# Adding the odd running sums of two units onto the even ones, clearing pads in part, and new engine orders in a gated linear attention with a ReGLU layer

## The chip, the core and the metric

One core of one Trainium2 chip runs the whole program. The metric is the device time of one execution in microseconds (us). Three executions of the kernel before took 193.5, 193.56 and 193.87 us: the median is 193.56 us.

## What is computed

For 4 sequences (batch B), 8 heads of width 48 and 768 tokens, a gated linear attention runs over the tokens, and its output, 3072 rows of 384, passes a ReGLU feed-forward layer:

```python
f = 1.0 / (1.0 + np.exp(-f_logit))
for t in range(S):
    state = f[:, :, t, :, None] * state + np.einsum('bhd,bhe->bhde', k[:, :, t], v[:, :, t])
    y[:, :, t] = np.einsum('bhd,bhde->bhe', q[:, :, t], state)
x = y.transpose(0, 2, 1, 3).reshape(B * S, H * D)
out = (np.maximum(x @ w_gate, 0.0) * (x @ w_val)) @ w_out     # 384 -> 1536 -> 384
```

Inputs and output are float32.

## The kernel before

The recurrence is worked in chunks of 128 tokens. Within a chunk, b(t) is the running sum of -log f, kept in bf16 as `bneg`; k is scaled by exp(b), q by exp(-b) (the "hats"), and masked products of the two give the part within the chunk, while a state of 48 x 48 per head carries the rest on. There are six groups c = 0 to 5 of four positions b = 0 to 3, 128 rows each, so 512 rows a group. Groups 0 and 1 are made of four **units**: a unit takes the first 256 tokens of one sequence, with tokens 2p and 2p+1 on partition p. Its two positions are the even tokens (b even) and the odd tokens (b odd). The change speaks of units 3 and 4: counted from zero they are 2 and 3, that is group 1, positions 0 and 1, and positions 2 and 3.

Every piece of work has a short name, which the text uses; digits are group and position:

- `Lf, Lk, Lq, Lv`: loads of an input (lines 406 and 411), 384 KB each. `wg0+2` and the like: loads of slices of w_gate, w_val, w_out from column block 0, two blocks (line 431, POOL queue).
- `ef`, `ln` (ACT, lines 478 and 481): exp, then log(1+x), for both positions of a unit at once.
- `cum` (PE, `cum2`, lines 492 to 500): the running sums, into one PSUM bank; the even position also sums the decays of its two chunks (line 498). `ek`, `eq` (ACT, 516 and 518) are the exponentials of the sums, `dc` (526) those of the decays. They read that bank.
- `hk`, `hq` (POOL or DVE, 540 and 541): k and q times the exponentials. `tk`, `tq` (PE, 552): their transposes; `ck`, `cq` (DVE or ACT, 556 and 557): the copies from PSUM.
- `s` (PE, 650): scores of a unit into four banks; `m` (DVE, 657): the masked copies. `y` (672), `yi` (708): outputs within and across chunks; `x` (597, ACT or DVE): their copy, the feed-forward layer's input. `v`: copy of v into `vpad` (570 to 572). `kv` (695), `st`, `ss`, `sd` (450 to 456): states.
- `g`, `u` (PE, 792): gate and value products of a hidden block j; `r` (ACT or DVE, 797 and 798): relu; `p` (DVE, 800): the product of the two. `o` (813), `d` (819 and 820), `S` (823): output product, copy, store. g00.2 is group 0, first position 0, block 2. Blocks 0 to 3 of group 0 are worked for two positions at a time (256 columns: g00.j, g02.j), all others for four (512 columns).

The order on each engine is written out in tables: `ORDER` lists operations by number for each engine, a negative entry ~7512 on PE means 7 products of 512 columns of zeros (line 877), which compute nothing. Before such a run, PE waits until the bank it writes is free. `BANKS` gives a bank for each accumulator in the order in which PE opens them. `HELD` adds waits: a load with a number in it waits until another has landed. All other waits follow from what an operation reads and writes; an operation that writes a bank waits for all readers of the bank's last use. The engines run these lists in order, so whatever waits holds all that stands behind it.

Of the kernel before, what the change touches and what calls it, by code (L numbers as in the profile page):

```python
# [14 lines left out]
X_WAY = "t" * 16 + "x" * 8  # L15
RUNS = {(c, b) for c in range(6) for b in (0, 2)}
# [8 lines left out]
        45, ~60100, 76, 87, ~4512, 84, ~3512, 92, 82, 103, ~2512, 94, 123, 112, 97, ~7512, 120, ~2512, 130, 102, 128, 106,  # L25
        118, 139, 158, 133, 154, 232, 243, ~3512, 150, 152, 146, 138, 279, 268, 142, 156, 160, 148, 174, 176, 170, 172, 186,
# [13 lines left out]
    ],  # L40
    "ACT": [
# [8 lines left out]
    ],  # L50
    "DVE": [
# [12 lines left out]
    ],  # L64
    "POOL": [
# [4 lines left out]
    ],  # L70
# [9 lines left out]
    51: 53, 57: 58, 59: 63, 63: 58, 65: 69, 67: 71, 70: 50, 71: 60, 72: 54, 517: 68,  # L80
# [161 lines left out]
def bass_hgrn2_outer__then__ffn_reglu_kernel(  # L242
# [10 lines left out]
    B, H, S, D = q.shape  # L253
# [106 lines left out]
    for i in range(NH):  # L360
        fill("DVE" if i < 3 else "POOL", f"hats{i}", hats[:, i, :, :, D:64], 0.0, 256, -14 + i)
    for i in range(NV):
        fill("POOL", f"vpad{i}", vpad[i][:], 0.0, VW, -8 + i)
# [95 lines left out]

    def halves(n, slot):  # L460
        return rows_of(n, slot).rearrange("p h (i d) -> p i h d", i=2)

    def front(c, b):
# [26 lines left out]
        bc = Bank("a")  # L490

        def cum2():
            for i in range(2):
                x = te.matmul(bc.ap[:, 0:HD], tsum[i * (1 - bj)][:, :], bneg[:, bi, i, :, 0:D], start=(i == 0), stop=(i == 1), skip_group_check=True)  # L494
            if bj == 0:
                for p in range(NP):
                    for i in range(2):
                        x = te.matmul(bc.ap[:, HD + 2 * p:HD + 2 * p + 2], bneg[:, bi, i, 2 * p:2 * p + 2, :].rearrange("p h d -> p (h d)"), pair[:, :],
                                      start=False, stop=(i == 1), skip_group_check=True)
            return x  # L500
# [442 lines left out]
```

## Time and profile before

| | before |
|---|---|
| median of three runs | 193.56 us |
| the profiled execution, whole | 193.41 us |
| its span, first to last instruction | 191.7 us |
| granted TensorE clock, mean | 1.000 |
| PE busy | 186.0 us in 2006 products |
| DVE, ACT, POOL busy | 146.7, 83.4, 60.0 us |

The profile is a page on one execution, taken by the hardware. Its other views, used below, are a timeline (start and length in us, engine, line, operation, shapes; behind a number in brackets, how long the engine had been idle and for whom it waited), busy times in chosen stretches, groups of instructions by line, and the chain of work that ended last, followed back. Lengths of neighbouring instructions of one engine overlap, since an engine is a pipeline: the distance from one start to the next is called a pitch below.

### The profile page before, as it was taken

To read this page: it belongs to the slowest core of one execution; us is meant where nothing else is said; L and a number is where in the kernel's file an instruction comes from. 1 tells how busy PE (TensorE), PEld (TensorE's weight loads), DVE (VectorE), ACT (ScalarE), POOL (GpSimd) and SP (SyncE) were. 2 spreads that over 40 slices of the span, in tenths; PEclk is the share of its full clock that TensorE was granted. 3 is DMA by queue.
4 is the path that set the end of the run, shared out by engine and by line. 5 is a ranking of instruction groups with operands and counts; after the bars stand their busy time and mean duration, and the time that the engine had idled before them with its cause. 6 is when DMAs were issued, how large, how long until landed. Compare 5 with 4: busy or idle time off the path is not lost.

```text
span 191.7 us, 4882 instructions
## 1 busy us (share of the span) xinstructions
PE 186.0 (97%) x2006; PEld 109.7 (57%) x2006; DVE 146.7 (77%) x264; ACT 83.4 (44%) x183; POOL 60.0 (31%) x92
## 2 busy tenths in 40 slices
PE   7899999999999999999999999999999999999994
PEld 7555675565645556655455755556555565555553
DVE  4469946999768989879986789996888947677331
ACT  2776963520387780472213996513351220222211
POOL 8899320201055820368200283911180000000000
DMA  5999999999989999899999999993239010000413
GB/s 149 325 285 261 206 208 278 204 225 279 241 185 193 225 212 208 160 187 255 204 162 220 238 203 236 176 202 79 64 120 180 20 41 3 2 0 0 164 44 123
DMA packets 110311, 32.44 MB, mean 169 GB/s; under 512 B 103504, under 2 KB 110032, under 8 KB 110288
## 3 DMA queue, kind: packets, MB, share of 16 engines
q1 hardware_dynamic: 95120, 25.44, 62.4%
q0 software_dynamic: 3776, 3.54, 11.4%
q10 hardware_dynamic: 11392, 3.15, 7.4%
q8 instruction: 16, 0.26, 0.6%
q14 instruction: 7, 0.06, 0.1%
HBM read 25.95 MB, written 4.72 MB: 160 GB/s over the span
## 4 chain that ended last, share of the span: by engine, by line
PE 75%; DMA 10%; DVE 5%; ACT 5%; issue 1%; POOL 1%; SPq 1%; ACTq 0%
PE ps L792 40%; PE ps L813 24%; DMA f_in<-in_f_logit_dram 7%; DMA wg<-in_moe_w_gate_dram 3%; PE ps L584 2%; DVE gT L800 2%; DVE hats L541 2%; PE ps L745 1%; PE ps L672 1%; PE ps L503 1%; POOL hats L540 1%; ACT f_in L478 1%; ACT expo L518 1%; PE ps L756 1%; ACT bneg L481 1%
## 5 line engine op out<-in xcount | busy, mean ns | idle before, releaser
L800 DVE TENSOR_TENSOR gT<-relu,ps 128x512 bf16<-128x512 bf16 (+1 forms) x76 | 48.5, 654 | 15.4 <-PE ps L792 11.4
L792 PE MATMUL ps<-xT,wg 128*128 128x512 bf16 (+1 forms) x228 | 57.8, 368 | 0.1
L792 PE MATMUL ps<-xT,wv 128*128 128x512 bf16 (+1 forms) x228 | 57.5, 368 | 0.0
L813 PE MATMUL ps<-wo,gT 128*128 128x384 bf16 (+2 forms) x300 | 51.9, 320 | 0.2 <-DVE gT L800 0.2
L797 ACT ACTIVATE relu<-ps 128x512 bf16<-128x512 f32 (+1 forms) x39 | 21.8, 565 | 46.2 <-PE ps L792 26.6
L813 PEld LDWEIGHTS ps<-wo,gT 128*128 128x128 bf16 x300 | 27.1, 98 | 18.4 <-DVE gT L800 1.2
L792 PEld LDWEIGHTS ps<-xT,wv 128*128 128x128 bf16 x228 | 23.6, 108 | 19.7 <-ACT expo L518 0.3
L792 PEld LDWEIGHTS ps<-xT,wg 128*128 128x128 bf16 x228 | 23.3, 108 | 19.1 <-DMA wg<-in_moe_w_gate_dram 0.6
L798 DVE TENSOR_SCALAR relu<-ps 128x512 bf16<-128x512 f32 (+1 forms) x37 | 24.8, 673 | 5.4 <-PE ps L792 4.4
L570 POOL CAST vpad<-v_in 128x384 bf16<-128x384 f32 x14 | 7.5, 550 | 43.6 <-PE ps L745 22.4
L592 DVE TENSOR_TENSOR ptm<-ps,tri 128x512 bf16<-128x512 f32 x32 | 19.9, 680 | 1.3 <-PE ps L584 1.3
L540 POOL TENSOR_TENSOR hats<-q_in,expo 128x384 bf16<-128x384 f32 x14 | 14.5, 1045 | 9.5 <-ACT expo L518 8.7
L478 ACT ACTIVATE f_in<-f_in 128x768 f32<-128x768 f32 x12 | 10.1, 845 | 14.1 <-DMA f_in<-in_f_logit_dram 14.0
L540 POOL TENSOR_TENSOR hats<-k_in,expo 128x384 bf16<-128x384 f32 x13 | 13.8, 1071 | 7.0 <-ACT expo L516 3.8
L456 POOL TENSOR_TENSOR st<-ssum,dec 128x384 bf16<-128x384 f32 x11 | 9.7, 878 | 16.1 <-DVE ssum L454 16.1
L518 ACT ACTIVATE expo<-ps 128x384 f32<-128x384 f32 x24 | 11.7, 492 | 4.2 <-PE ps L503 2.9
L597 ACT ACTIVATE xT<-ps 128x384 bf16<-128x384 f32 x10 | 5.4, 548 | 16.9 <-PE ps L672 8.3
L516 ACT ACTIVATE expo<-ps 128x384 f32<-128x384 f32 x24 | 11.6, 493 | 1.1 <-PE ps L494 0.6
L819 ACT ACTIVATE osb<-ps 128x384 f32<-128x384 f32 (+1 forms) x15 | 7.3, 483 | 10.3 <-PE ps L813 9.8
L657 DVE TENSOR_TENSOR ptm<-ps,tmask 128x512 bf16<-128x512 f32 x16 | 10.2, 681 | 1.2 <-PE ps L650 1.1
L877 PE MATMUL ps<-zeros 128*128 128x100 bf16 (+1 forms) x81 | 10.6, 307 | 0.0
L481 ACT ACTIVATE bneg<-f_in 128x768 bf16<-128x768 f32 x12 | 10.1, 842 | 0.2
(78 smaller groups left out, 169.8 us busy)
## 6 DMA issues: line engine op xcount, KB each, us to landing
out_dram<-osb SPq DMA_DIRECT2D x23, 192.0 KB, 2.4
f_in<-in_f_logit_dram SPq DMA_DIRECT2D x11, 384.0 KB, 5.9
k_in<-in_k_dram SPq DMA_DIRECT2D x11, 384.0 KB, 5.7
q_in<-in_q_dram SPq DMA_DIRECT2D x10, 384.0 KB, 5.7
v_in<-in_v_dram SPq DMA_DIRECT2D x8, 384.0 KB, 5.1
v_in<-in_v_dram ACTq DMA_DIRECT2D x4, 384.0 KB, 6.4
q_in<-in_q_dram ACTq DMA_DIRECT2D x2, 384.0 KB, 6.5
wg<-in_moe_w_gate_dram POOLq DMA_DIRECT2D x2, 384.0 KB, 8.8
```

What stands on the lines that cost most here:

```text
L478: add(f"ef{c}{b0}", by("ACT", lambda: sc.activation(raw, raw, AF.Exp, scale=-1.0), act_(n)), keys, keys, key=P)
L481: add(f"ln{c}{b0}", by("ACT", lambda: sc.activation(bo, fl, AF.Ln, bias=1.0), act_(n)), keys + [f"bneg{bi}"], [f"bn{bi}_{x % 2}" for x in ...
L516: add(f"ek{c}{b}", by("ACT", lambda: sc.activation(ex[:, 1, :], bc.ap[:, 0:HD], AF.Exp, scale=1.0), act_(HD)), [bc], [f"expk{ei}"], key=P + 1)
L518: add(f"eq{c}{b}", by("ACT", lambda: sc.activation(ex[:, 0, :], bc.ap[:, 0:HD], AF.Exp, scale=-1.0), act_(HD)), [bc], [f"expq{ei}"], key=P ...
L540: return {**by("POOL", lambda: gp.tensor_tensor(o, i_, e_, ALU.mult), pool_(HD)), **by("DVE", lambda: ve.tensor_tensor(o, i_, e_, ALU.mult ...
L592: add(f"m{c}{b}{j}", by("DVE", lambda b=b, j=j, mi=mi: ve.tensor_tensor(ptm[mi][:, j, :, :], s[b, j].ap[:, :].rearrange("p (n t) -> p n t" ...
L792: z = te.matmul(bank.ap[:, 0:n], wt[:, kt, w_cols(j)], xT[xi][:, kt, n0:n1], start=(kt == 0), stop=(kt == NK - 1))
L797: add(f"r{c}{b0}.{j}", {**by("ACT", lambda: sc.activation(rdst, gate.ap[:, 0:n], AF.Relu), act_(n)), **by("DVE", lambda: ve.tensor_scalar_ ...
L798: **by("DVE", lambda: ve.tensor_scalar_max(rdst, gate.ap[:, 0:n], 0.0), dve_(n))}, [gate], [f"relu{ri}"], key=P)
L800: add(f"p{c}{b0}.{j}", by("DVE", lambda: ve.tensor_tensor(gT[gi][:, j, n0:n1], rdst, val.ap[:, 0:n], ALU.mult), dve_(n)), [val, f"relu{ri} ...
L813: z = te.matmul(o.ap[:, 0:e1 - e0], gT[gi][:, j, b * C:(b + 1) * C], wo[:, j, e0:e1], start=(j == 0), stop=(j == NJ - 1))
L877: te.matmul((op.opens[0].ap if op.opens else banks[7])[:, 0:fill % 1000], zeros[:, 0:128], zeros[:, 0:fill % 1000], start=True, stop=True, ...
```

## The change

For units 3 and 4, the sums of the odd tokens are no longer two products into a bank of their own (sum of the even gates and sum of the odd gates up to the token). One product with the identity adds the odd gates onto the even sums, in the bank where these lie. It stands behind all readers of the even sums (`ek`, `eq` and `dc`), since it overwrites what they read. w_out stays in its four slices (`WO` is as it was). Of `vpad`, only the 64 columns of pads that no copy fills are cleared, not all 448, still on POOL; all six `hats` pads are cleared on DVE, where three were POOL's. All five orders, `BANKS` and `HELD` are new.

```diff
+ONTO = {2, 3}
...
-        fill("DVE" if i < 3 else "POOL", f"hats{i}", hats[:, i, :, :, D:64], 0.0, 256, -14 + i)
+        fill("DVE", f"hats{i}", hats[:, i, :, :, D:64], 0.0, 256, -14 + i)
...
-        fill("POOL", f"vpad{i}", vpad[i][:], 0.0, VW, -8 + i)
+        fill("POOL", f"vpad{i}", vpad[i][:].rearrange("p (n e) -> p n e", n=NP)[:, :, D:64], 0.0, 64, -8 + i)
...
-        bc = Bank("a")
+        onto = two and bj and w // 2 in ONTO
+        bc = sums_at[w // 2] if onto else Bank("a")
+        sums_at[w // 2] = bc
         def cum2():
+            if onto:
+                return te.matmul(bc.ap[:, 0:HD], ident[:, :], bneg[:, bi, 1, :, 0:D], start=False, stop=True, skip_group_check=True)
...
-            add(f"cum{c}{b}", pe(cum2, mm(HD) * 2 + (mm(2) * 8 if bj == 0 else 0)), ["tsum0", "tsum1", "pair", f"bneg{bi}", f"bn{bi}_0", f"bn{bi}_1"],
-                [bc], key=P, opens=[bc])
+            add(f"cum{c}{b}", pe(cum2, mm(HD) if onto else mm(HD) * 2 + (mm(2) * 8 if bj == 0 else 0)),
+                ["ident", f"bneg{bi}", f"bn{bi}_1"] if onto else ["tsum0", "tsum1", "pair", f"bneg{bi}", f"bn{bi}_0", f"bn{bi}_1"],
+                [bc], key=P, opens=[] if onto else [bc])
```

The orders are given by name up to the place where both kernels have done the same work on PE. PE before, then after:

```
warm ~60x100 cum00 cum01 ~4 tq00 ~3 tk01 tk00 kv00 ~2 tq01 cum03 cum02 s00 ~7 tq02 ~2 tq03 y00 tk03 yi01 tk02 kv02
  g00.3 s02 g00.2 cum10 cum11 ~3 g00.1 u00.1 g00.0 y02 cum13 cum12 yi03 u00.2 u00.3 u00.0 | g02.3 u02.3 ...
warm ~60x100 cum00 cum01 ~7 tq00 ~2 tq01 tk00 tk01 kv00 ~5 cum02 s00 cum03 ~3 tq02 ~2 tq03 ~1 y00 yi01 tk02 tk03 kv02
  g00.3 s02 g00.2 g00.0 u00.0 ~3 cum10 g00.1 u00.1 cum12 y02 u00.3 u00.2 yi03 cum11 cum13 | g02.1 g02.0 u02.0 g00.4 g02.3
  u02.3 tq12 g00.7 u02.1 u00.4 g00.5 u00.7 u00.5 g02.2 u02.2 g00.6 u00.6 ~1 tk10 ~1 g00.8 ...
```

Here ~7 stands for 7 empty products of 512 columns. Behind the bar PE has no empty products before, and two after. The other engines in the same stretch, after:

```
ACT  ef00 ln00 dc00 eq00 eq01 ek01 ek00 cq00 ef02 ck01 ln02 ck00 eq02 dc02 ek02 eq03 ek03 cq02 x01 ck02 ef10 ln10 r00.2
     ef12 r00.0 ln12 eq10 ek10 dc10 r00.1 eq12 dc12 x02 ek12 x03 eq11 ek11 ...
DVE  ... hk00 hk01 cq01 st00 ss10 v03 sd10 m000 m011 m001 m010 cq03 hk02 hk03 x00 ck03 st01 r00.3 ss11 m031 m030 m021
     p00.0 m020 p00.1 p00.3 p00.2 ...
POOL ... wg2+2 ... v01 v00 hq00 hq01 wo0+2 wv0+2 v02 wg0+2 hq02 hq03 wv2+2 wg4+4 sd11 wv4+4 wv8+4 wg8+4 ...
SP   Lf0.0 Lq0.0 Lf0.2 Lv0.2 Lk0.2 Lf1.0 Lf1.2 Lq1.2 Lk1.0 Lq1.0 Lk1.2 Lk2.0 Lv3.2 ...
```

and before:

```
ACT  ef00 ln00 eq00 dc00 ek01 eq01 ek00 ef02 ck01 ln02 ek03 v03 eq02 eq03 dc02 ek02 cq03 x00 ef10 ln10 ef12 r00.3 ek10 eq11
     dc10 eq10 r00.2 ek11 ln12 r00.0 x02 ek12 eq12 dc12 ...
DVE  ... v01 v00 al1 hq00 cq00 hk00 ck00 st00 ss10 cq01 m010 m011 m000 m001 cq02 hk03 hk02 ck03 x01 ck02 st01 ss11 m031 sd11
     m030 m020 m021 r00.1 p00.1 x03 ...
POOL ... wg2+2 mvpad4 hk01 hq01 wo0+2 wv0+2 sd10 v02 hq02 hq03 wg0+2 wv2+2 wg4+4 wv4+4 wv8+4 wg8+4 ...
SP   Lf0.0 Lq0.0 Lf0.2 Lv0.2 Lk0.2 Lf1.0 Lf1.2 Lq1.2 Lk1.0 Lq1.0 Lk1.2 Lk3.2 ...
```

Two waits between loads are gone with `HELD`: before, Lk1.0 stood behind the landing of wv4+4, and Lk1.2 behind that of wv8+4. At the end, PE before closes with o53.8b, o53.4a and o53.8a (256 of the last position's columns), after with o51 and o52 whole (384 columns); the last copy before is d53a, after d52, both on ACT.

More of the change, by code (lines that the diff above doesn't have):

```diff
@@ L24 @@
     "PE": [
-        45, ~60100, 76, 87, ~4512, 84, ~3512, 92, 82, 103, ~2512, 94, 123, 112, 97, ~7512, 120, ~2512, 130, 102, 128, 106,
-        118, 139, 158, 133, 154, 232, 243, ~3512, 150, 152, 146, 138, 279, 268, 142, 156, 160, 148, 174, 176, 170, 172, 186,
[13 rows of a table removed]
+        45, ~60100, 76, 87, ~7512, 84, ~2512, 94, 82, 92, 103, ~5512, 112, 97, 123, ~3512, 120, ~2512, 130, ~1512, 102, 106,
+        118, 128, 139, 158, 133, 154, 146, 148, ~3512, 232, 150, 152, 268, 138, 160, 156, 142, 243, 279, 166, 162, 164, 178,
+        174, 176, 276, 190, 168, 180, 182, 192, 184, 170, 172, 186, 188, ~1512, 238, ~1512, 194, 202, 248, 204, 240, 206,
[12 rows of a table added]
     ],
     "ACT": [
[8 rows of a table removed]
[8 rows of a table added]
     ],
     "DVE": [
[12 rows of a table removed]
[12 rows of a table added]
     ],
     "POOL": [
[4 rows of a table removed]
[4 rows of a table added]
     ],
     "SP": [
[4 rows of a table removed]
[4 rows of a table added]
     ],
@@ L79 @@
 HELD = {
-    51: 53, 57: 58, 59: 63, 63: 58, 65: 69, 67: 71, 70: 50, 71: 60, 72: 54, 517: 68,
+    51: 55, 57: 53, 63: 64, 67: 71, 70: 47, 71: 60, 515: 73,
 }
 BANKS = [
[9 rows of a table removed]
[9 rows of a table added]
 ]
@@ L458, in new_state @@
                 [key] + dk, [f"S{b}_{c % 2}"], key=P + 8)
+    sums_at = {}
     def halves(n, slot):
```

99 rows, old and new, of tables (BANKS, ORDER) are left out of this document.

## Prediction

> **What bounds the kernel now.** I read the busy times of the page first, then those of the stretch behind 26.12 us, then those of the empty products alone in the stretch ahead of 21.94.
>
> ```profile
> PE 186.0 (97%) x2006; PEld 109.7 (57%) x2006; DVE 146.7 (77%) x264; ACT 83.4 (44%) x183; POOL 60.0 (31%) x92
> ```
> ```profile
> 26.12:188.97 162.85, 162.41 (x1574) 93.22 (x1571) 129.07 (x214) 64.89 (x143) 40.81 (x49) 1.00 0.78 158
> ```
> ```profile
> 7.02:21.94 14.92, 5.53 (x21) 1.80 (x21) 1.00 1.25 270
> ```
>
> PE's 97% is two things. From 26.12 us to 188.97 it is busy 162.41 of 162.85 us, and by the order none of that is empty products: this part is worth its work, and little can be gained there. From 7.02 to 21.94 all 21 empty products of 512 columns take 5.53 busy us; there PE waits for a chain through ACT, POOL, DVE and loads. So the time after the change is: when PE reaches the place where the work behind 26.12 begins (g02.3 before, g02.1 after; by the two orders the work ahead of it is the same but for the product saved twice), the work behind it, empty products and waits in it, and the tail. The granted clock is 1.00 in both stretches.
>
> **The start, to g00.3.** The timeline of the start, by engine, and one piece of the chain that ended last:
>
> ```profile
> 5.16 0.84 ACT L478 ACTIVATE f_in<-f_in 128x768 f32<-128x768 f32 x1 [3.06 <-DMA f_in<-in_f_logit_dram]
> 7.72 0.49 ACT L518 ACTIVATE expo<-ps 128x384 f32<-128x384 f32 x1 [0.85 <-PE ps L498]
> 8.11 0.36 ACT L526 ACTIVATE dec<-ps 64x8 f32<-64x8 f32 x2
> 10.25 0.84 ACT L478 ACTIVATE f_in<-f_in 128x768 f32<-128x768 f32 x1 [0.52 <-DMA f_in<-in_f_logit_dram]
> 11.00 0.58 ACT L557 ACTIVATE qkT<-ps 128x512 bf16<-128x512 bf16 x1
> 11.48 0.83 ACT L481 ACTIVATE bneg<-f_in 128x768 bf16<-128x768 f32 x1
> 9.05 1.00 POOL L540 TENSOR_TENSOR hats<-k_in,expo 128x384 bf16<-128x384 f32 x1 [0.89 <-ACT expo L516]
> 10.01 1.32 POOL L540 TENSOR_TENSOR hats<-q_in,expo 128x384 bf16<-128x384 f32 x1
> 9.77 0.70 DVE L541 TENSOR_TENSOR hats<-k_in,expo 128x384 bf16<-128x384 f32 x1
> 13.99 2.48 DVE L657 TENSOR_TENSOR ptm<-ps,tmask 128x512 bf16<-128x512 f32 x4 [1.10 <-PE ps L650]
> 18.10 0.58 DVE L597 CAST xT<-ps 128x384 bf16<-128x384 f32 x1
> 13.30 0.64 PE L650 MATMUL ps<-qkT 48*64 48x128 bf16 x32
> 16.61 0.73 PE L672 MATMUL ps<-ptm,vpad 64*32 64x128 bf16 x64
> 18.27 0.52 PE L695 MATMUL ps<-vpad,hats 64*128 64x96 bf16 x16
> 18.74 0.50 PE L792 MATMUL ps<-xT,wg 128*128 128x256 bf16 x3
> ```
> ```profile
> 34.09 0.22 PE ps L552 x4
> ```
>
> After, dc00 goes ahead of eq00, so eq00 runs from 8.10 to 8.59, and both q hats go to POOL: hq00 from 8.65 to 9.65 (1.00, the row at 9.05). hq01 follows at 9.6, beside hk00 and hk01 on DVE; POOL's row at 10.01 ran beside DVE's at 9.77 and took 1.32. With it hq01 ends at 10.9, with 1.00 at 10.6; I take 10.9. (The Trainium skill, GPSIMD Engine Reference, 1. Specifications, says that the two engines share their interfaces to SBUF and contend where a DVE instruction has two SBUF inputs, as hk00 and hk01 have; so it too points to the longer row, and with the shorter the start would be 0.3 us earlier.)
>
> Three transposes at a pitch of 0.22 (the chain that ended last has one set of four so) end at 11.8, so ck01 starts at 11.87, against 11.00 before. It stands ahead of ln02 on ACT: ln02 runs 12.35 to 13.2, 0.87 late. cum02 at 13.26, its 0.60 (the row pair at 20.09 and 20.69 below), and s00 at 13.86, 0.56 late; ck00, now on ACT behind ln02, ends at 13.7, inside that. The masked copies start 0.69 after s00, as before, and end 2.48 later at 17.03; y00 at 17.15, 0.54 late. Then, on DVE, cq03, hk02 and hk03 (which ran before the masks or among other work) hold tk03 until 18.55, and one transpose and kv02 (0.47, 18.27 to 18.74) later g00.3 starts at 19.25, **0.5 us late**.
>
> The clears cost nothing and gain nothing: ACT idled 3.06 us for f_logit up to 5.16, and the first sums stand behind that. But POOL, freed of them, issues wg2+2 some 2.5 us earlier, beside this load:
>
> ```profile
> 1.94 8.29 DMA f_in<-in_f_logit_dram
> 6.73 0.95 POOL L431 DMA_DIRECT2D wg<-in_moe_w_gate_dram  x1
> ```
>
> It landed at 10.23. ln02 now waits for ck01 anyhow, so ef02 (0.75 to the next start, 10.25 to 11.00) may begin as late as 11.1: 0.9 us of cover. I price it at nothing, and at 0.5 us if the cover is gone.
>
> **From g00.3 to g02.1.**
>
> ```profile
> 20.09 0.50 PE L494 MATMUL ps<-bneg,tsum 128*128 128x384 bf16 x2
> 20.69 0.50 PE L494 MATMUL ps<-bneg,tsum 128*128 128x384 bf16 x2
> 21.02 0.81 PE L877 MATMUL ps<-zeros 128*128 128x512 bf16 x3
> 21.94 0.50 PE L792 MATMUL ps<-xT,wg 128*128 128x256 bf16 x3
> 25.13 1.16 PE L792 MATMUL ps<-xT,wv 128*128 128x256 bf16 x9
> 26.12 0.49 PE L792 MATMUL ps<-xT,wg 128*128 128x256 bf16 x3
> 17.40 0.61 ACT L597 ACTIVATE xT<-ps 128x384 bf16<-128x384 f32 x1
> 17.86 0.83 ACT L478 ACTIVATE f_in<-f_in 128x768 f32<-128x768 f32 x1
> 18.72 0.84 ACT L481 ACTIVATE bneg<-f_in 128x768 bf16<-128x768 f32 x1
> ```
>
> Before, 18.74 to 26.12 is 7.38 us, of which 0.92 from the start of the three empty products at 21.02 to 21.94. So the common work is 6.46, and less two products of 0.16 (half of the 0.33 from 20.69 to 21.02) 6.13. Were PE never held, after needs 19.25 + 6.13 + 0.65 for its three empty products (21.02 to 21.67, where the wait for wg0+2 began) = 26.03. But it is held twice. The empty products wait for m031, which DVE reaches behind x00, ck03, st01, r00.3 and ss11: from 19.0 (ck03 waits for tk03) 0.36, then 0.55, 0.38, 0.47 and 0.68 to its end, estimates from DVE's rows above (a 384-wide one takes 0.58, a masked copy 0.62): 21.45. PE is there by 21.26 (1.35 from 18.74 to 20.09 for g00.3, s02 and g00.2, then two more at 0.33, a third of 25.13 to 26.12). So cum10 starts at 22.15, behind 0.65 of empty products. From there to the end of yi03 is the stretch 21.94 to 26.12 less g00.0, u00.0 and cum13 (0.99), with cum10 (0.60) in their place: 4.18 - 0.99 + 0.60 = 3.79, so it ends at 25.9. Then g02.1 needs x03, which is now ACT's: 0.61 by the row at 17.40 and some 0.1 of handing over, 26.6.
>
> ACT says the same from its side. From x01 at 18.26 (behind yi01) it has, by pitches: x01 and x02 0.46 (17.40 to 17.86), ck02 0.48 (11.00 to 11.48), ef10 0.86 (17.86 to 18.72, its ln waits for its end), ln10, ef12 and ln12 0.75 (10.25 to 11.00), four exponentials of sums 0.39 (7.72 to 8.11), two dc 0.37, and three relus of 256 columns, an estimate of 0.28 from the 384-wide 0.39: 7.6 us, so x03 starts at 25.9 and ends at 26.5. ek12 ends at 26.0, so cum13, which now waits for it, stands perhaps 0.1 us, with g02.1 behind it, which waits for x03 longer. So **the two saved products (0.33) vanish here**: both stand between yi03 and g02.1, where PE waits. g02.1 at 26.6 against 26.12: **+0.5**.
>
> **Behind it.** Two single empty products around tk10. hk10 is on DVE behind p02.2, which follows u02.2; two DVE instructions of about 0.5 us stand against g00.6 and u00.6 on PE, 1.3 us, so hk10 is there first, nothing hides the empty products, and they cost 0.22 each (a third of 0.65), **+0.43**, bounds 0 to 0.43. The two waits of PE behind 26.12 are
>
> ```profile
> 42.02 0.64 PE L650 MATMUL ps<-qkT 48*64 48x128 bf16 x32 [0.21 <-DVE qkT L556]
> 125.66 0.82 PE L813 MATMUL ps<-wo,gT 128*128 128x384 bf16 x4 [0.21 <-DVE gT L800]
> ```
>
> At the first, s12 waits for copies on DVE; after, s10 comes first and two of those copies are on ACT: **-0.21**. I leave the second. The work that moves between engines here (on balance POOL has three hats more and three v copies less, ACT four v copies more, DVE three hats less and three output copies more) is hidden while each engine keeps ahead of PE; DVE, busy 129.07 of 162.85 us, has the least room.
>
> **The tail.** The last store was 256 columns and will be 384.
>
> ```profile
> L823 SPq DMA_DIRECT2D out_dram<-osb x7: 332/332/333, 179.7 to 189.5; - x7
> DMA to landing us min/median/max: 1.6/1.8/1.9
> ```
> ```profile
> L819 ACT ACTIVATE osb<-ps 128x384 f32<-128x384 f32 x14 | 6.9, 491 | 9.2 <-PE ps L813 8.7 <-DMA out_dram<-osb 0.5
> L819 ACT ACTIVATE osb<-ps 128x256 f32<-128x256 f32 x1 | 0.4, 384 | 1.1 <-PE ps L813 1.1
> ```
>
> The copy is 491 - 384 ns = 0.11 longer, the landing some 0.15: **+0.25**.
>
> **Sum.** 0.5 + 0.43 - 0.21 + 0.25 = +0.97 us on the profiled 193.41, 194.4. The median of the runs lies 0.15 above that execution, so 194.5.
>
> **The rivals.** *The start closes up* (faster). If the 1.32 is 1.00, ACT's small ones come faster and m031 and x03 are never late, g00.3 is back at 18.74 and g02.1 at 18.74 + 6.13 + 0.65 = 25.52, -0.60. With one of the late empty products standing in a true wait (+0.22), both waits of 0.21 gone and the tail: -0.60 + 0.22 - 0.42 + 0.25 = -0.55, 193.0. It decides once x03 ends before 26.0. For it: PE had 0.92 us of emptiness here; against: two chains, DVE's and ACT's, both give 26.5. 0.21.
>
> *The start's delay holds only in part* (no change): g02.1 at 26.12, one empty product hidden, -0.21 and the tail: +0.26, 193.8. 0.15.
>
> *Weights come late* (slower than forecast).
>
> ```profile
> L431 POOL DMA_DIRECT2D wg<-in_moe_w_gate_dram x4: 772/796/946, 6.7 to 20.1; - x4
> DMA to landing us min/median/max: 5.7/6.7/10.5
> ```
> ```profile
> 18.52 1.55 POOL L431 DMA_DIRECT2D wv<-in_moe_w_val_dram  x2
> 26.70 0.37 SPq L406 DMA_DIRECT2D k_in<-in_k_dram  x1
> ```
>
> wv4+4 was issued at 18.52; after, it stands on POOL behind sd11, which waits for ss11, so 21.7. k1.0, held until 26.70 before, and q1.0, k1.2 and k2.0 are now on SP's queue right behind q1.2, among the weights. u00.4 needs wv4+4 at 26.6 + 3.5 = 30.1 (six blocks of 256 columns at 0.33, two of 512 at 0.65, a transpose). If it lands within 8.4 us nothing is lost; at the longest 10.5 it is there at 32.2, 2.1 us late. Three fifths of that, 1.3, give 195.8. (By the Trainium skill, DMA: Bandwidth & Descriptors, Queues, rings and completion order, each DMA engine takes its queues in turn, a packet at a time, so the inputs would slow the weights though they are issued elsewhere; no run here shows the four inputs so placed.) 0.16.
>
> **How the numbers follow.** The forecast has 0.48, its own range 194.0 to 195.1. Faster and slower than no change begin at 0.2%, some 0.4 us, about what can be told here. Faster: the first rival, 0.21. Same: the second and a thin edge of the forecast, 0.16. Slower: 0.63. The range runs from the first rival's 193.0 to the third's 195.8.
>
> **What would show it.** Right: g00.3 near 19.25, PE idle ahead of g02.1 with x03 on ACT as releaser, no gain of the saved products, tk10 ready before its empty product ends, a last store of 192 KB. Wrong: g02.1 at or before 26.12; a wait of PE for wv or wg near 30 us; new waits between 45 and 170 us, where I found none.

## The result and the profile after

| | before | after |
|---|---|---|
| median | 193.59 us (8 runs) | 194.36 us (8 runs) |
| lowest and highest | 193.35, 194.02 | 193.80, 194.74 |
| the profiled execution, whole | 193.41 | 194.19 |
| its span | 191.7 | 192.5 |
| ratio of the times | | 1.0036, 95% interval 1.0022 to 1.0049 |

The change costs 0.77 us, against 0.94 forecast for the medians. Ratios here and below weigh the executions without those more than 1.5% above the fastest of their kernel, which count as slow (one of all_mended, three of all_mended_apart), so a ratio is not the quotient of the medians, which take all executions. First the page's busy times (PEld is PE's loading of weights), the stretch from g02.1 to PE's end, and the empty products in that stretch. A row for a stretch gives its length, then the busy time and the number of instructions of PE, PEld, DVE, ACT and POOL, then the granted clock, the DMA engines' busy share and GB/s; the last row counts PE and PEld of the empty products' line alone:

```profile
PE 184.4 (96%) x1991; PEld 109.3 (57%) x2008; DVE 142.1 (74%) x266; ACT 85.1 (44%) x184; POOL 56.8 (29%) x89
27.02:189.50 162.48, 161.34 (x1560) 93.78 (x1574) 125.37 (x215) 65.80 (x143) 39.98 (x47) 1.00 0.75 156
27.02:189.50 162.48, 0.76 (x2) 0.20 (x2) 1.00 0.75 156
```

PEld counts 2008 weight loads, PE 1991 products: 17 records of products are missing, so PE's busy times after read a little low, and the places are read from starts. The order of work behind g02.1 is as tight as before: 162.48 us against 162.85, though two empty products now stand in it. The loss is ahead of it. The timeline of the start, after:

```profile
11.60 0.84 ACT L482 ACTIVATE f_in<-f_in 128x768 f32<-128x768 f32 x1 [0.78 <-DMA f_in<-in_f_logit_dram]
12.35 0.58 ACT L567 ACTIVATE qkT<-ps 128x512 bf16<-128x512 bf16 x1
12.82 0.83 ACT L485 ACTIVATE bneg<-f_in 128x768 bf16<-128x768 f32 x1
3.65 0.94 POOL L433 DMA_DIRECT2D wg<-in_moe_w_gate_dram  x1
8.72 1.96 POOL L550 TENSOR_TENSOR hats<-q_in,expo 128x384 bf16<-128x384 f32 x2 [1.85 <-ACT expo L528]
9.82 1.75 DVE L551 TENSOR_TENSOR hats<-k_in,expo 128x384 bf16<-128x384 f32 x2 [4.13 <-ACT expo L526]
14.32 0.64 PE L660 MATMUL ps<-qkT 48*64 48x128 bf16 x32
17.73 0.73 PE L682 MATMUL ps<-ptm,vpad 64*32 64x128 bf16 x64
19.81 0.39 PE L802 MATMUL ps<-xT,wg 128*128 128x256 bf16 x2
26.08 0.78 PE L501 MATMUL ps<-bneg,ident 128*128 128x384 bf16 x2
26.35 0.61 ACT L607 ACTIVATE xT<-ps 128x384 bf16<-128x384 f32 x1
27.02 0.83 PE L802 MATMUL ps<-xT,wg 128*128 128x256 bf16 x6 [0.15 <-ACT xT L607]
83.90 0.99 PEld L802 LDWEIGHTS ps<-xT,wg 128*128 128x128 bf16 x6
84.14 1.02 PE L802 MATMUL ps<-xT,wg 128*128 128x512 bf16 x4 [0.29 <-ACT xT L607]
```

wg2+2 is issued at 3.65 instead of 6.73, and ef02 starts at 11.60 instead of 10.25, its wait ending with the load of f. ck01 follows right behind it at 12.35 and ln02 at 12.82; s00 is 1.02 late (14.32 against 13.30), g00.3 1.07 (19.81 against 18.74). The contention of the hats shows on the other engine than foreseen: the two on POOL take 0.98 each, the two on DVE 1.75 together, where the one beside POOL's took 0.70 before. g02.1 starts at 27.02, 0.90 behind the place that g02.3 had before, with PE idle for x03 on ACT (26.35 to 26.96). Behind it, the two waits of before, at s12 and o33.0, are gone, and one at g20.2, shown as 0.29 at 84.14, is new. It is shown too long: the first product of g20.2 is one of the missing records. Its weights are loaded at 83.90, as the row of PEld shows, so it started some 0.2 us ahead of 84.14.

### The profile page after: what moved, and what is told of

Same layout as the page of the kernel before. It is cut to its first block, busy times and chain, and to the rows that moved or that the text cites. A ratio compares the mean times of both kernels' runs of the same rounds, so it can differ in the third digit from the quotient of the medians.

```text
span 192.5 us, 4857 instructions
## 1 busy us (share of the span) xinstructions
PE 184.4 (96%) x1991; PEld 109.3 (57%) x2008; DVE 142.1 (74%) x266; ACT 85.1 (44%) x184; POOL 56.8 (29%) x89
## 3 DMA queue, kind: packets, MB, share of 16 engines
q0 software_dynamic: 3776, 3.54, 11.1%
## 4 chain that ended last, share of the span: by engine, by line
PE 82%; ACT 6%; DMA 5%; DVE 3%; issue 1%; SPq 1%; POOL 1%; DVEq 0%
PE ps L802 44%; PE ps L823 25%; DMA f_in<-in_f_logit_dram 5%; PE ps L594 2%; PE ps L755 2%; DVE gT L810 2%; PE ps L512 1%; ACT bneg L485 1%; ACT f_in L482 1%; PE ps L562 1%; PE ps L782 1%; PE ps L682 1%; ACT xT L607 1%; ACT expo L528 1%; PE ps L766 1%
## 5 line engine op out<-in xcount | busy, mean ns | idle before, releaser
L802 PE MATMUL ps<-xT,wv 128*128 128x512 bf16 (+1 forms) x225 | 56.8, 368 | 0.2
L802 PE MATMUL ps<-xT,wg 128*128 128x512 bf16 (+1 forms) x217 | 55.2, 367 | 1.0 <-ACT xT L607 0.4
L550 POOL TENSOR_TENSOR hats<-q_in,expo 128x384 bf16<-128x384 f32 x17 | 17.2, 1019 | 38.7 <-ACT expo L528 34.3
L550 POOL TENSOR_TENSOR hats<-k_in,expo 128x384 bf16<-128x384 f32 x13 | 12.9, 1000 | 17.7 <-ACT expo L526 15.5
L458 POOL TENSOR_TENSOR st<-ssum,dec 128x384 bf16<-128x384 f32 x11 | 9.0, 830 | 15.6 <-DVE ssum L456 15.6
L830 DVE COPY osb<-ps 128x384 f32<-128x384 f32 (+1 forms) x13 | 6.8, 534 | 8.6 <-DMA out_dram<-osb 4.8
L829 ACT ACTIVATE osb<-ps 128x384 f32<-128x384 f32 (+1 forms) x12 | 5.7, 485 | 14.3 <-PE ps L823 11.2
L456 DVE TENSOR_TENSOR ssum<-ps,st 128x384 f32<-128x384 f32 x16 | 8.8, 555 | 1.7 <-PE ps L782 1.3
```

The source lines that it names most:

```text
L550: return {**by("POOL", lambda: gp.tensor_tensor(o, i_, e_, ALU.mult), pool_(HD)), **by("DVE", lambda: ve.tensor_tensor(o, i_, e_, ALU.mult ...
L802: z = te.matmul(bank.ap[:, 0:n], wt[:, kt, w_cols(j)], xT[xi][:, kt, n0:n1], start=(kt == 0), stop=(kt == NK - 1))
```

## Experiments

Each kernel is the kernel after with one edit, unless its text says otherwise. They ran in four groups, each on a chip of its own, with the kernel before beside them: wg_later, before_wg_early, no_late_zeros and tail_256 (its median there 193.59 us); two_products, before_onto, hats_swapped and all_mended (193.71); after_again, loads_apart and all_mended_apart (193.62); k3_early (193.75). A range behind a median is the lowest and highest time; an edit shown in part ends in "...". Tables hold operations by number; the text gives their names.

### The start: the early weights

wg_later puts wg2+2 (56) behind v00 (86) on POOL again:

```diff
+o = ORDER["POOL"]
+o.remove(56)
+o.insert(o.index(86) + 1, 56)
```

> The changed kernel, with the first weight load wg2+2 moved on POOL behind the two v copies v01 and v00, so that it is issued at about 6.9 us, as in the kernel before (6.73), not at 3.65. Theory A (the weights issued early hold up the second f load, and this is part of the late start): Lf0.2 lands near 10.2 us, not 11.55; ef02 starts near 10.7; but ln02 still stands behind ck01, which waits for tk01 until 12.0, so ln02 comes only 0.3 us earlier (12.5) and g00.3 at 19.5, not 19.81; time about 0.3 us less than the changed kernel, ratio to before near 1.002. Rival B (the load alone makes the late start): g00.3 at 18.9, time 0.9 us less, ratio near 0.999. Rival C (the early issue has nothing to do with the landing): Lf0.2 lands near 11.5 as it does now, ratio stays 1.0036.

before_wg_early is the kernel before with wg2+2 ahead of POOL's first clears (13):

```diff
+o = ORDER["POOL"]
+o.remove(56)
+o.insert(o.index(13), 56)
```

> The kernel before, with wg2+2 moved forward on POOL, ahead of the second clear of tsum, so that it is issued at about 3.6 us and not at 6.73. Nothing else is changed. Theory A: Lf0.2 lands near 11.5 us, not 10.23; ef02, ck01 and ln02 follow at once there, so g00.3 comes about 1.2 us later, near 19.9; wg0+2, which stands on POOL behind hq02 and hq03, lands later too, so nothing absorbs it: time 1.0 to 1.2 us more, 194.7, ratio 1.005 to 1.006. Rival C (issue time does not matter): ratio 1.000, Lf0.2 at 10.2.

Timelines, the first three lines of wg_later, the other three of before_wg_early:

```profile
6.94 0.50 PE L508 MATMUL ps<-bneg,tsum 128*128 128x384 bf16 x2 [0.99 <-ACT bneg L490]
12.45 0.83 ACT L490 ACTIVATE bneg<-f_in 128x768 bf16<-128x768 f32 x1
19.47 0.50 PE L807 MATMUL ps<-xT,wg 128*128 128x256 bf16 x3
```
```profile
11.42 0.84 ACT L483 ACTIVATE f_in<-f_in 128x768 f32<-128x768 f32 x1 [1.70 <-DMA f_in<-in_f_logit_dram]
19.91 0.50 PE L797 MATMUL ps<-xT,wg 128*128 128x256 bf16 x3
27.29 0.49 PE L797 MATMUL ps<-xT,wg 128*128 128x256 bf16 x3
```

One transfer of weights, issued 3 us earlier on another engine's queue, holds f back by 1.2 us in the kernel before (ef02 at 11.42 instead of 10.25); g00.3 and g02.3 (27.29 instead of 26.12) come 1.17 later. (By the Trainium skill, DMA: Bandwidth & Descriptors, Queues, rings and completion order, a DMA engine serves its queues in turn, a packet at a time, so an early issue on one queue takes time from the others; the trace agrees in the effect, with these 1.2 us.) The time is 194.90, ratio 1.0060 (1.0045 to 1.0076). In the kernel after the same delay is worth some 0.2: without it g00.3 stands at 19.47, 0.34 earlier, and ln02 at 12.45, where the chain through the hats holds it. But 0.11 of the 0.34 lies ahead of the weights' effect, since the first sums start at 6.94 instead of 7.05, and in after_again, a second execution of the kernel after whose first sums start at 6.94 too, g00.3 stands at 19.65, 0.18 behind wg_later. The effect was so shown both ways. But wg_later as a whole took 195.43 us, ratio 1.0082 (1.0054 to 1.0110), though its g02.1 came 0.29 earlier than in the kernel after. Its six executions lie in the range that the kernel after shows itself when run again (below), so they do not tell the two apart; where its profiled execution lost time is taken up below too.

### The saved products

two_products makes the odd sums of units 3 and 4 by two products again, in the same banks and places:

```diff
+ONTO = set()
+BANKS[38:38] = [5, 0]
```

> The kernel after with the odd sums of units 3 and 4 made again by two products into their bank, the first of which wipes it: PE has two products of 0.16 us more, at the same places and behind the same waits. Theory A (the saved products vanished, since both stand ahead of g02.1, which waits for x03 on ACT, idle 0.15): the 0.33 goes half into that wait, so g02.1 at 27.0 to 27.25 and the time 0 to 0.2 above the kernel after's 194.4. Rival B (they were a true gain): g02.1 at 27.35, the time up by 0.33, and no idle of PE for x03.

The stretch of yi03, the sums and g02.1, in a second execution of the kernel after (after_again, below), then in two_products:

```profile
25.82 0.35 PE L718 MATMUL ps<-qkT,st 128*32 128x128 bf16 x12
26.10 0.60 PE L501 MATMUL ps<-bneg,ident 128*128 128x384 bf16 x2
26.87 0.83 PE L802 MATMUL ps<-xT,wg 128*128 128x256 bf16 x6 [0.17 <-ACT xT L607]
```
```profile
25.85 0.35 PE L722 MATMUL ps<-qkT,st 128*32 128x128 bf16 x12
26.13 0.82 PE L507 MATMUL ps<-bneg,tsum 128*128 128x384 bf16 x4
26.91 0.83 PE L806 MATMUL ps<-xT,wg 128*128 128x256 bf16 x6
```

From yi03 to g02.1 it is 1.05 us with the two single products of the change and 1.06 with four: the 0.33 saved is all wait. The median is 194.57, against 194.36 and 194.67 of the kernel after. Theory A's direction holds, and the loss is even less than its half of 0.33.

before_onto is the kernel before with the ONTO lines of the diff, and:

```diff
+move("PE", 243, 138)
+move("PE", 279, 178)
+for op, ahead in ((234, 235), (245, 141), (244, 141)):
+    move("ACT", op, ahead)
...
```

`move` puts one operation ahead of another in an engine's list. These are cum11 ahead of y02, cum13 ahead of g00.4, eq10 ahead of dc10, and eq11 and ek11 ahead of x02; the banks are fitted to that order.

> The kernel before with the odd sums of units 3 and 4 added on by one product each, and nothing else of the change: cum11 moved ahead of y02, cum13 behind the first blocks of g02, the exponentials reordered on ACT to fit. Theory A (a saved product is worth its time only where PE has no wait behind it): cum11 leaves the stretch ahead of g00.1, which waits for weights until 21.94 anyhow, so nothing is gained there and its one product costs 0.16 later; cum13 saves 0.33 - 0.16: the time 0 to -0.2 against before. Rival B (both are worth their 0.16): -0.33. A third: the exponentials come later for one of the hats, and PE waits for a transpose of group 1 near 35 us: +0.2 or more.

It took 193.60 against 193.71, ratio 0.9991 (0.9979 to 1.0003). Its trace shows the first half of theory A, in

```profile
22.02 0.50 PE L816 MATMUL ps<-xT,wg 128*128 128x256 bf16 x3 [0.27 <-DMA wg<-in_moe_w_gate_dram]
```

g00.1 waits for its weights until 22.02 (21.94 before), so what cum11 frees ahead of it is lost. Whether the rest is worth 0.1 or 0.3 us the times can't tell; from the first sums to the end its profile is some 0.3 us shorter than that of the kernel before (191.5 less 7.11 against 191.7 less 7.02), one execution each.

### The late empty products and the tail

no_late_zeros leaves out the two empty products around tk10 (238) and g00.8 (194):

```diff
+del o[o.index(238) - 1], o[o.index(194) - 1]
```

> The changed kernel without the two single empty products around tk10. If tk10's hats are ready before PE is there, as forecast: 0.43 us less than the changed kernel, ratio to before near 1.0014, no idle time of PE ahead of tk10 or g00.8. If they cover true waits: no change, ratio 1.0036, and PE shows idle time of some 0.2 us at one of the two.

Timeline of PE, after and then without them:

```profile
35.05 0.38 PE L887 MATMUL ps<-zeros 128*128 128x512 bf16 x1
35.27 0.39 PE L562 MATMUL ps<-ident,hats 128*128 128x128 bf16 x4
35.49 0.38 PE L887 MATMUL ps<-zeros 128*128 128x512 bf16 x1
35.70 0.38 PE L802 MATMUL ps<-xT,wg 128*128 128x512 bf16 x1
```
```profile
35.01 0.39 PE L566 MATMUL ps<-ident,hats 128*128 128x128 bf16 x4
35.24 1.03 PE L806 MATMUL ps<-xT,wg 128*128 128x512 bf16 x4
124.31 0.50 PE L516 MATMUL ps<-bneg,tri 128*128 128x384 bf16 x2
```

g00.8 follows tk10 at once, and no wait takes their place there: 0.23 from 35.01 to 35.24, where it was 0.65 from 35.05 to 35.70, so in their place they cost 0.42. Not all of it reaches the end. cum51, at 124.31, starts 1.50 behind the six products ahead of it (122.81), in the kernel after 1.30 (123.25 to 124.55): it stands for a load of f through ACT, and gives 0.2 back. The profiled span, 192.1, is 0.4 below that of the kernel after, but after_again has 192.1 with both empty products. The median (194.43, 193.43 to 196.06; ratio 1.0050, 1.0027 to 1.0074) doesn't show it, because the executions spread.

tail_256 restores the tail of before: o51 and o52 ahead of the parts of o53, with the copies, stores and banks to match.

```diff
+o[-11:] = [915, 916, 917, 920, 921, 922, 931, 932, 925, 926, 927]
...
```

> The changed kernel, with the last output products in the order of the kernel before: o51 and o52 whole, then position 3's parts, so that the last store is of 256 columns, 128 KB. Theory: the stretch from PE's end to the span's end shrinks from 2.98 to 2.73 us, time 0.25 us less, ratio to before near 1.0023. Rival: PE waits at the end for a copy or a bank, no gain.

195.06 (193.69 to 196.23), ratio 1.0067 (1.0043 to 1.0090). In its profile DVE's hq12 takes 1.23 us instead of 0.55, as POOL's hk11 runs beside it, and PE waits at tq12:

```profile
28.42 1.23 DVE L558 TENSOR_TENSOR hats<-q_in,expo 128x384 bf16<-128x384 f32 x1
28.24 0.99 POOL L557 TENSOR_TENSOR hats<-k_in,expo 128x384 bf16<-128x384 f32 x1 [4.02 <-DMA k_in<-in_k_dram]
29.70 0.40 PE L569 MATMUL ps<-ident,hats 128*128 128x128 bf16 x4 [0.49 <-DVE hats L558]
190.73 0.38 ACT L836 ACTIVATE osb<-ps 128x256 f32<-128x256 f32 x1 [1.33 <-PE ps L830]
```

(The Trainium skill, GPSIMD Engine Reference, 1. Specifications, has the two engines contend for SBUF where a DVE instruction has two SBUF inputs; the trace agrees, with 0.55 alone and 1.23 beside it.) The tail's gain can't be told from such times, but its profile shows it: the last copy starts at 190.73, 2.6 us ahead of the end of the span (193.3), against 2.9 in the kernel after.

### Why the executions spread

The kernel before stays mostly within 193.3 and 194.2; no_late_zeros, tail_256 and two_products ran from 193.4 to 196.4. Two explanations were tried against each other. hats_swapped takes the collision away: hq12 (273) to POOL, hk11 (246) to DVE behind p00.4.

```diff
+ORDER["DVE"].remove(273)
+ORDER["DVE"].insert(ORDER["DVE"].index(183), 246)
+o = ORDER["POOL"]
+o[o.index(246)] = 273
```

> The kernel after with two hats exchanged between engines: hq12 on POOL, in hk11's place, and hk11 on DVE behind p00.4. Theory A (the kernel after is held in many executions by DVE's hq12, which takes 1.13 to 1.23 us where it runs beside POOL's hk11, and 0.55 where not, so tq12 comes 0.55 to 0.65 late on PE): no wait of PE at tq12 in any profile, the executions nearer together, the median 0.2 to 0.5 below the kernel after's 194.4. Rival B (the spread is from loads that land late, whatever the hats): the spread stays and the median is within 0.2.

195.23 (194.20 to 196.56), ratio 1.0081 (1.0054 to 1.0108): the spread stays, so the collision isn't its cause. It is itself a sign of k1.0 landing at about 28.1 (in tail_256) instead of 26.6 (in the kernel after).

after_again is the kernel after, unchanged.

> The kernel after itself, unchanged, beside the next two on the same chip. Theory A (its own executions scatter like those of its variants, since four inputs are on SP's queue among the weights and the order of landings changes from one execution to the next): lowest 193.8 or below, highest 195.5 or above, median 194.3 to 194.8. Rival B (only the variants scatter): all within 193.8 to 194.8.

194.67 (193.98 to 196.22), ratio 1.0063 (1.0036 to 1.0091): the spread is the kernel's own, though the first eight executions stayed within 193.80 and 194.74. Over both sets its 17 times have a median of 194.53.

loads_apart places weights and inputs as before: wv4+4, wv8+4 and wg8+4 ahead of sd11 (144), and the two holds.

```diff
+o = ORDER["POOL"]
+o.remove(144)
+o.insert(o.index(68) + 1, 144)
+HELD.update({59: 63, 65: 69})
```

> The kernel after with the transfers placed as before: wv4+4, wv8+4 and wg8+4 issued ahead of sd11 on POOL (at about 18.7 us instead of 22.1), k1.0 behind the landing of wv4+4 and k1.2 behind that of wv8+4. Theory A (the spread comes from inputs and weights competing between 15 and 32 us): highest less lowest falls to about 0.9 as before (193.3 to 194.2), the median to 194.0 or a little below; the start and the late empty products still cost what they cost. Rival B (the spread is from hats on POOL beside those on DVE, or the order of the copies): the spread stays above 1.5.

194.50 (194.03 to 196.54), ratio 1.0051 (1.0026 to 1.0076): a miss. The weights were issued at 21.18, not 18.7, since HELD also makes wv4+4 wait for f1.2, which I had overlooked. But its profile is of a long execution (195.67) and shows where the time goes. Timelines of loads_apart; then of the kernel after, of the kernel before:

```profile
81.47 2.65 SPq L419 DMA_DIRECT2D k_in<-in_k_dram  x2
87.92 0.99 POOL L556 TENSOR_TENSOR hats<-k_in,expo 128x384 bf16<-128x384 f32 x1 [2.58 <-DMA k_in<-in_k_dram]
89.06 0.33 PE L788 MATMUL ps<-vpad,hats 128*128 128x96 bf16 x4 [1.00 <-POOL hats L556]
```
```profile
79.62 2.49 SPq L413 DMA_DIRECT2D k_in<-in_k_dram  x2
85.20 1.01 POOL L550 TENSOR_TENSOR hats<-k_in,expo 128x384 bf16<-128x384 f32 x1
```
```profile
30.60 1.14 SPq L411 DMA_DIRECT2D k_in<-in_k_dram  x1
```

This is k3.2, for hk32 and kv32. Before, it was issued at 30.60, 50 us ahead of its use. The change moved it on SP's queue behind the stores S10 and S11. There it is issued at 79.6 in the short executions, lands 4.5 us later and is needed by POOL at 85.2; in loads_apart, where it is issued 1.9 us later and takes 6.3 us to land, PE loses about 1 us at kv32. wg_later shows the same at 88.95 (idle 0.42), but there it is one place of several: by the starts of PE's weight loads, against after_again, kv32 costs 1.2 of the 1.7 us that loads_apart loses, 0.6 of 1.6 in wg_later and 0.3 of 1.5 in tail_256, while tq12, behind k1.0, costs 0.6 and 0.7 in these two.

The last three put together what had a price. all_mended: wg2+2 behind v00, the hats swapped, no late empty products, the tail of 256 columns, and

```diff
+o = ORDER["PE"]
+o.remove(142)
+o.insert(o.index(138) + 1, 142)
+o.remove(279)
+o.insert(o.index(166) + 1, 279)
+ORDER["ACT"].remove(145)
+o = ORDER["DVE"]
+o.insert(o.index(161), 145)
```

which is yi03 ahead of u00.3, cum13 behind g02.1, and x03 from ACT to DVE.

> The kernel after with what the runs so far put a price on taken out: wg2+2 issued behind v00, the two hats exchanged as in hats_swapped, the two late empty products left out, a tail of 256 columns, and the stretch ahead of g02.1 reordered: yi03 ahead of u00.3, x03 on DVE ahead of p00.3, cum13 behind g02.1. Theory: g02.1 at 26.3 instead of 27.0 (-0.3 by the load of f, -0.4 by x03), -0.43 by the empty products, -0.25 by the tail, and the waits at tq12 gone: 192.6 to 193.1, below both kernels. Rival: an earlier start runs into later loads (waits at kv32 or o41.0), and the time stays at 193.5 or above.

195.02 (193.75 to 197.00), ratio 1.0050 (1.0027 to 1.0074): the rival. In its profile g02.1 stands at 25.91, 1.1 earlier than in the kernel after, and then the weights of u00.4 aren't there:

```profile
25.91 0.49 PE L826 MATMUL ps<-xT,wg 128*128 128x256 bf16 x3
30.56 0.81 PE L826 MATMUL ps<-xT,wv 128*128 128x512 bf16 x3 [0.84 <-DMA wv<-in_moe_w_val_dram]
```

wv4+4 lands at about 30.2 in the kernel after (issued at 22.14, and 8.1 us on the way), and its u00.4 starts at 30.51. The start can close up by some 0.3 us (0.1 in after_again) before this transfer takes the wait over.

all_mended_apart takes all_mended, without the exchange of the hats, and adds the two edits of loads_apart.

> all_mended with the transfers as in loads_apart, and the two hats left as in the kernel after: wg2+2 behind v00, weights ahead of sd11, the two holds, no late empty products, a tail of 256 columns, yi03 ahead of u00.3, x03 on DVE ahead of p00.3, cum13 behind g02.1. Theory A: no wait of PE at u00.4 (0.84 in all_mended), g02.1 near 26.4, 192.7 to 193.2, below both kernels and with a small spread. Rival: the holds make k1.0 or k1.2 late for the hats (tk11 or tk12 waits near 36 us), 193.5 or above.

194.67 (192.82 to 196.26), ratio 1.0036 (1.0010 to 1.0063). Its profiled execution took 193.10, with a span of 191.4, and there the prices add up: no wait at u00.4, g02.1 at 25.81, and only tq10 late. So its shortest executions are below both kernels, its median is not.

k3_early is all_mended_apart with k3.2 (517) in the place of v4.2 (661) on SP's queue, the loads for groups 4 and 5 behind k3.0 (513), and wv4+4 waiting for f1.0 instead of f1.2:

```diff
+HELD[63] = 58
+o = ORDER["SP"]
+a, b = o.index(517), o.index(661)
+o[a], o[b] = o[b], o[a]
+for op in (660, 801, 661):
+    o.remove(op)
+    o.insert(o.index(513) + 1, op)
```

> all_mended_apart with the loads of group 3 earlier: k3.2 takes the place of v4.2 on SP's queue, behind f3.0 (at about 62 us, where it stood at 79 to 81.5), v4.2, k5.0 and q4.2 go behind k3.0, and wv4+4 waits for the landing of f1.0 instead of f1.2, so that the weights are issued near 18.7 and not at 21.1. Theory A (the spread of the kernel after comes mostly from k3.2, issued so late that in many executions hk32 on POOL and with it kv32 on PE wait for it, 0.28, 0.58 and 1.15 us in the slow profiles): no wait at kv32, highest less lowest 1.2 or less (3.4 in all_mended_apart), median 192.8 to 193.4, below before's 193.6. Rival B (the spread has other places: hq12, tq10, o41.0, g20.2): the spread stays above 2 and the median at 194 or above, though kv32 never waits.

194.33 (192.83 to 195.26), ratio 1.0020 (1.0000 to 1.0040). The profiled execution is its longest, 195.26:

```profile
84.71 1.01 POOL L581 TENSOR_TENSOR hats<-k_in,expo 128x384 bf16<-128x384 f32 x1
118.59 1.51 SPq L444 DMA_DIRECT2D f_in<-in_f_logit_dram  x1
123.84 0.84 ACT L513 ACTIVATE f_in<-f_in 128x768 f32<-128x768 f32 x1 [2.50 <-DMA f_in<-in_f_logit_dram]
125.95 0.50 PE L543 MATMUL ps<-bneg,tri 128*128 128x384 bf16 x2 [1.28 <-ACT bneg L516]
```

POOL no longer waits for k3.2, and nothing is lost at kv32. The spread falls from 3.4 to 2.4 us, not to 1.2, on another chip and with twelve executions each, so the fall itself is not shown to come from the edit. Now the last load of f for group 5, f5.0, issued at 118.59 (115.20 in the profile of the kernel after, 114.56 in that of all_mended_apart), holds cum51, where PE stands 1.28 us. Theory A is right on the place and wrong that it is the main one; rival B's clause holds, though with another place than those it named. What the long executions shown here share is that loads land late, and the first one without slack makes PE wait. With issue and time to landing together, k1.0 lands at 28.1 in tail_256 and at 27.9 in wg_later (26.6 in the kernel after), k3.2 at 87.4, 87.7 and 87.8 in tail_256, wg_later and loads_apart (84.1), f5.0 at 123.8 in k3_early (121.5). SP's queue is late at k3.2, by 1.7 to 1.9 us in these three, but not at k1.0, issued at 16.20 in tail_256 and at 14.14 in wg_later against 15.78: there the way is longer. Why loads come late in one execution and not in the next stays open, and no variant of the kernel after has a median below that of the kernel before.

## Why the prediction was right, and where it was not

The forecast was +0.97 on the profiled 193.41, it came to +0.78: 194.19. The direction and the time hold, though two terms were mis-sized, in opposite directions: g02.1 came 0.90 late where 0.48 was forecast, and the work behind it got 0.37 shorter where it should have got 0.22 longer. That the sum is off by no more than 0.19 is so in part luck.

- **The start, +0.5 forecast, +1.07 measured.** From ck01 on the chain named (ck01 ahead of ln02, s00, masks, tk03) is the one that the trace shows. Ahead of ck01 the trace has the load of f and ef02 in place of the hats; these hold ck01 once the load is not late, as in wg_later, at 11.95. What failed is "I price it at nothing, and at 0.5 us if the cover is gone" for the early wg2+2: ef02 came at 11.60, beyond the 11.1 that I allowed. The price of the lost cover was well bounded, some 0.2 by wg_later; the cover was taken as given, although the one load beside the transfer could be seen landing at 10.23, with 0.9 us of room. The remaining 0.3 is spread over the hats and the steps around s00; no run takes it apart. The hats' contention fell on DVE (1.75 for two), where I had put it on POOL (1.32 for hq01).
- **From g00.3 to g02.1, 7.35 forecast, 7.21 measured.** cum10 at 22.59, x03 last, PE idle for it by 0.15: the step holds, and two_products shows that the saved products vanish there.
- **The two late empty products, +0.43.** In their place this held; no_late_zeros shows 0.42 there. At the end leaving them out is worth 0.2 less, by cum51.
- **The waits behind, -0.21 forecast.** The wait at s12 went as forecast, the one that I left, at 125.66, went too. Each was also worth more than its idle time. In the row order of PE before and after,

```profile
124.64 0.81 PE L792 MATMUL ps<-xT,wv 128*128 128x512 bf16 x3
125.66 0.82 PE L813 MATMUL ps<-wo,gT 128*128 128x384 bf16 x4 [0.21 <-DVE gT L800]
```
```profile
34.40 0.81 PE L802 MATMUL ps<-xT,wv 128*128 128x512 bf16 x3
35.05 0.38 PE L887 MATMUL ps<-zeros 128*128 128x512 bf16 x1
```

  three such products take 0.65 from start to start where nothing is waited for, and 1.02 ahead of the wait: 0.37 each, since idle time begins only at the modelled end of the last product. So -0.74 where I had -0.21, and +0.2 for the new wait at g20.2, which stands for x (0.3 from the four short products ahead of it, at 83.61, to its first one, where such four take 0.1). The starts leave 0.2 to 0.3 more of gain, in steps of a tenth that I did not trace.
- **The tail, +0.25.** As forecast: the last copy, of 384 columns, starts at 189.60, 2.9 us ahead of the end of the span; before, that of 256 started at 189.05, 2.65 ahead. Before, then after:

```profile
189.05 0.38 ACT L819 ACTIVATE osb<-ps 128x256 f32<-128x256 f32 x1 [1.11 <-PE ps L813]
```
```profile
189.60 0.49 ACT L829 ACTIVATE osb<-ps 128x384 f32<-128x384 f32 x1 [1.46 <-PE ps L823]
```

- **Weights come late.** It did not happen in the kernel after, by some 0.3 us at u00.4; all_mended shows the same transfer holding PE once the start is 1.1 us earlier. The first rival, that the start closes up, was so tied to the third: the prediction treated them as apart.
- **What I did not see.** k3.2's move on SP's queue. I followed the loads to 31 us and looked for new waits behind 45 us only on the engines. The forecast named new waits between 45 and 170 us as what would make it wrong; the one at g20.2 stands in the profiled execution itself, the larger ones in the long executions.

## What to carry to other kernels

Price a transfer that is issued earlier by what lands later, on every queue, and read a load's slack (landing to first use) before and after for each load that an order moves, to the end of the kernel and not only around the edit. Work taken away just ahead of an engine's wait is worth nothing; its price is the start of the next instruction, so compare starts at equal arrival. When a start is shortened, look for the next transfer with less slack than the gain, and take several executions: one profile shows one order of landings.

## What was not expected of the hardware

- A weights transfer on POOL's queue, 3 us earlier, made a load on SP's queue, issued ahead of it at 1.93, land 1.2 to 1.3 us later.
- A hat on DVE takes 0.55 alone and 1.13 (wg_later) or 1.23 (tail_256) beside a hat on POOL, while POOL's stays at 0.99; two on DVE beside two on POOL take 1.75 together.
- A wait of PE shown as 0.21 us idle costs 0.37 from start to start.
- SP's issues themselves spread: k3.2 leaves at 79.6 in one execution and at 81.5 in another of nearly the same order, and takes 4.5 us to land in the one, 5.9 in the other. Executions of one order of work then differ by up to 2.2 us (193.98 and 196.22 in after_again), with the clock at 1.00 in both.
